# A fused retention and two-layer MLP kernel on one core: another order of its opening, another rate of weight conversion for layer 2, and a whole last output block

## The chip, the cores and the metric

The kernel runs on one core of a Trainium2 chip. The metric is device time in microseconds (us) from launch to end, as a median of several runs; the profile gives the span from the first to the last instruction of one execution, which is a little shorter. PE is TensorE (matmuls), DVE is VectorE, ACT is ScalarE, POOL is GpSimd, SP is SyncE, which here only issues DMAs.

## The reference

Retention over 2 sequences with 8 heads, 768 positions and head width 64, then two feed-forward layers over the 1536 resulting rows of width 512. Both hidden widths are 2048.

```python
gamma = 1.0 - 2.0 ** (-5.0 - np.arange(H))
for t in range(S):
    state = gamma * state + outer(k[:, :, t], v[:, :, t])
    y[:, :, t] = (1 / sqrt(D)) * einsum('bhd,bhde->bhe', q[:, :, t], state)
x = y.transpose(0, 2, 1, 3).reshape(B * S, H * D)
h = x @ moe_w_in;   x = elu(h) @ moe_w_out
h = x @ moe2_w_in;  out = softplus(h) @ moe2_w_out
```

q, k and v are float32, the four weight matrices are float64 in memory, the output is float32.

## The kernel before

**Retention by tiles.** The 1536 positions are 12 tiles of 128, six to a sequence; four tiles make a block of 512 rows. A tile j goes through these helpers. `load_tile` (L68) issues three DMAs of 256 KB on SP's queue, q, k and v. `ret_prep` (L197) scales v by a decay, on DVE for the first four tiles and on POOL for the rest. `ret_transpose` (L201) transposes q and k on PE, four 128x128 pieces each; DVE then copies q out of PSUM while it multiplies by the query decay `gq` (L216), and ACT copies k out (L214). `ret_scores` (L243) forms the 128x128 score blocks of the eight heads in 16 matmuls, and DVE multiplies them by the causal mask into the tile A (L252), of which there is one buffer. `ret_state` (L225) forms k'v in 16 matmuls, and DVE folds it into the running state `st` (L237 to L240). `ret_wide` (L219) has POOL copy that state into a block-diagonal tile `wide`. `ret_out` (L256) is eight matmuls of `wide` (not for the first tile of a sequence) and 16 of A with v into one bank; ACT writes the rounded high half xh (L276) and DVE the rest xl (L277).

**Matrix products by units.** 96 units follow: 2 layers, 3 blocks of 512 rows, 16 slices of 128 hidden columns. Every operand is split into a high part, rounded by ACT, and a low part, subtracted by DVE (`split_w`, L158 to L167, for weights; `act_split`, L325, for activations), and each product is three passes. `hidden(u)` (L293) is 12 matmuls of 512 columns: w_hi x_hi, w_hi x_lo, w_lo x_hi. `act(u)` (L303) is ELU in layer 1 (two ACT and one DVE instruction) and softplus in layer 2 (three ACT and four DVE). `project(u)` (L333) is another 12 matmuls into four accumulators. In the loop over u at L452, `hidden` and `act` run two units ahead of `project`. In layer 1 one retention job of a tile 4 to 11 (transposes, scores, or output with state) is put in each unit from u = 1 on.

**Weights.** `load_w` (L128) brings a 128x512 float64 slice (512 KB) into one of five `raw` buffers; `conv_w` (L139) turns it into float32 with two ACT instructions (L150, L151) and two DVE instructions (L152, L153). `wq` (L379) is the order of the slices, and `next_conv` (L393) converts the next slice if its place is free and then issues the load of one more. A layer-2 slice becomes free when the last block of layer 1 has split the layer-1 slice in that place, from u = 29 on. In a unit the first `next_conv(1)` stands behind `hidden`, and a second call stands at the unit's end (L467): always for layer-1 weights, and for layer-2 weights only if u is even.

**Order of the work.** Nothing is scheduled by a planner: each engine runs its instructions in the order in which the program lists them, and DMAs of one queue are issued in program order. The opening is the code from L399 to L439. SP issues tiles 0 and 1 (L85, L86), then a weight slice, tile 2, a slice, tile 3, three slices, tiles 4 and 5. In the opening the masks (L252) of tile s-1 are multiplied between the two transposes of tile s, and `ret_out(s - 1)` comes in the same step:

```python
    for s in range(TPB):
        ret_transpose(s, (0,))
        ...
        if s:
            ret_scores(s - 1)
        ret_transpose(s, (1,))
        ret_wide(s)
        ret_state(s)
        ...
        if s:
            ret_out(s - 1)
```

`gq` is made on the chip: ACT's queue loads 2x512 decays and a 2x128 selector, one matmul (L115) spreads them over 128 partitions, DVE copies the result. `keep_clock` (L106) issues matmuls on a zeroed tile, 8 at the start and 4 in the first step of the opening. At the end `finish` (L353) copies the four output blocks of 128 rows out of PSUM, ACT for even and DVE for odd ones, the very last one in two halves, one by each engine, and SP's queue writes them out.

Of the kernel before, what the change touches and what calls it, by code (L numbers as in the profile page):

```python
# [19 lines left out]
P = 128  # L20
# [3 lines left out]
def tile_retention_elu_softplus(  # L24
# [43 lines left out]
    def load_tile(j):  # L68
        b, c = divmod(j, CPB)
        r = []  # L70
        for n, (src, nm) in enumerate(((q, "q"), (k, "k"), (v, "v"))):
            t = early[n][:, j] if j < TPB else rp.tile([P, H, D], F32, tag=nm, name=nm)
            nc.sync.dma_start(out=t, in_=src[b, :, c * P:(c + 1) * P, :].rearrange("h s d -> s h d"))
            r.append(t)
        qkv[j] = r
# [3 lines left out]
    decq = gp.tile([2, HP * P], F32, tag="gh", name="decq")  # L79
    sel = gp.tile([2, P], F32, tag="gl", name="sel")  # L80
    dec = const.tile([P, H + HP], F32, name="dec")
    nc.scalar.dma_start(out=decq, in_=decay_q[:, 0:HP * P])
    nc.scalar.dma_start(out=sel, in_=decay_q[:, HP * P:])
    nc.scalar.dma_start(out=dec, in_=decay)
    load_tile(0)  # L85
    load_tile(1)  # L86
# [23 lines left out]
    keep_clock(8)  # L110


    gq = const.tile([P, HP * P], F32, name="gq")
    gb = ps.tile([P, 512], F32, tag="r1", name="gb")
    nc.tensor.matmul(gb, sel, decq, start=True, stop=True)  # L115
    nc.vector.tensor_copy(gq, gb)
# [80 lines left out]
    def ret_prep(j):  # L197
        vt = qkv[j][2]
        (nc.vector if j < TPB else nc.gpsimd).tensor_tensor(out=vt, in0=vt, in1=gv, op=ALU.mult)
# [43 lines left out]
    def ret_scores(j):  # L243
# [6 lines left out]
        a = ap.tile([P, 2, HP, P], F32, tag="A", name="A")  # L250
        for i in range(2):
            nc.vector.tensor_tensor(out=a[:, i], in0=bs[i].rearrange("p (h t) -> p h t", h=HP),  # L252
                                    in1=mask.unsqueeze(1).to_broadcast([P, HP, P]), op=ALU.mult)
        scores[j] = a

    def ret_out(j):  # L256
# [11 lines left out]
        for pr in range(HP):  # L268
            for i in range(2):
                o = i * D  # L270
                nc.tensor.matmul(b[o:o + D, pr * P:(pr + 1) * P], vt[:, 2 * pr + i, :], a[:, i, pr, :],  # L271
# [21 lines left out]
    def hidden(u):  # L293
# [4 lines left out]
        seq = [(ah, xh, kk) for kk in range(KK)] + [(ah, xl, kk) for kk in range(KK)] + [(al, xh, kk) for kk in range(KK)]  # L298
# [53 lines left out]
    def finish(u):  # L352
# [3 lines left out]
        for i in range(4):  # L356
# [4 lines left out]
            else:  # L361
                o = rp.tile([P, DM], F32, tag="qk"[i // 2], name="o")
                r = blk * TB + i * P
                if u == NU - 1 and i == 3:
                    nc.scalar.activation(out=o[:, :DM // 2], in_=acc[i][:, :DM // 2], func=AF.Copy)
                    nc.vector.tensor_copy(o[:, DM // 2:], acc[i][:, DM // 2:])
                elif i % 2:
# [3 lines left out]
                nc.sync.dma_start(out=out[r:r + P, :], in_=o)  # L371
# [26 lines left out]

    next_load(1)  # L399
    load_tile(2)  # L400
    next_load(1)
    load_tile(3)
    next_load(3)
    load_tile(4)
    load_tile(5)
    cv = list(wq)

    for s in range(TPB):
        ret_transpose(s, (0,))
        if s == 0:  # L410
            ret_prep(0)
        if s:
            ret_scores(s - 1)
        ret_transpose(s, (1,))
        ret_wide(s)
        ret_state(s)
        if s == 0:
            keep_clock(4)
        ret_prep(s + 1)
        if s:  # L420
            next_conv(1)
        if s > 1:
            split_w(s - 2, 0)
        if s:
            ret_out(s - 1)
    ret_scores(TPB - 1)
    ret_wide(TPB)
    ret_out(TPB - 1)
    rot["banks"] = ["r0", "r1"]
# [9 lines left out]
    next_conv(1)  # L439
# [12 lines left out]
    for u in range(NU):  # L452
# [14 lines left out]
        if not cv or cv[0][0] == 0 or u % 2 == 0:  # L467
# [3 lines left out]
def _decay(H, D):  # L471
    gamma = [1.0 - 2.0 ** (-5.0 - h) for h in range(H)]
    HP = H // 2
    d = np.zeros((P, H + HP), dtype=np.float32)
    dq = np.zeros((2, HP * P + P), dtype=np.float32)
    for h, g in enumerate(gamma):
        d[D * (h % 2):D * (h % 2 + 1), H + h // 2] = g ** P
        dq[h % 2, HP * P + D * (h % 2):HP * P + D * (h % 2 + 1)] = 1.0
        for t in range(P):
            d[t, h] = g ** -(t + 1)  # L480
            dq[h % 2, P * (h // 2) + t] = g ** (t + 1) / float(D) ** 0.5
    return d, dq
# [28 lines left out]
```

## Time and profile before

| what | value |
|---|---|
| time, median of 3 runs | 604.85 us (603.58 to 986.68) |
| the profiled execution's own time | 605.01 us |
| its span | 602.5 us |
| busy in the span: PE, DVE, ACT, POOL | 591.9, 466.5, 415.5, 22.4 us |
| mean granted TensorE clock | 0.995 |

The profile is of one execution. Its own time is 2.5 us longer than its span (start and end outside the instructions), and 0.16 us above the median. Busy time of an engine is the time in which at least one of its instructions ran; matmuls overlap, so a busy PE need not be PE at its full rate.

### The profile page before, as it was taken

The page shows a single profiled execution, that of the slowest core. Times are in us where ns is not written, and L with a number is a line of the kernel's source. Part 1 is how long each engine was busy: PE and PEld are TensorE (multiplying, and loading weights), DVE is VectorE, ACT ScalarE, POOL GpSimd, SP SyncE. Part 2 cuts the span into 40 slices and gives each one's busy share as a digit, 9 for nine tenths or more (in the row PEclk, how much of TensorE's full clock was granted, in tenths as well). Part 3 has the DMA queues.
Part 4 walks back from the last instruction along what each step waited for, and adds up shares of the span by engine and source line. Part 5 has one row for each costly group of instructions (what it writes and reads, how often), then busy time and mean ns, then how long its engine had stood idle before and what let it go on. Part 6 is the DMA issues. An engine that isn't in the chain of part 4 may idle for free.

```text
span 602.5 us, 8184 instructions
## 1 busy us (share of the span) xinstructions
PE 591.9 (98%) x3038; PEld 484.1 (80%) x3038; DVE 466.5 (77%) x746; ACT 415.5 (69%) x700; POOL 22.4 (4%) x38
## 2 busy tenths in 40 slices
PE   8999999999999999999999999999999999999997
PEld 4777888888888888888888877888888888888885
DVE  3969999865655545888888999978877887878774
ACT  1569888844644456898888977766776667766763
POOL 1200100110111000000000000000000000000000
PEclk9989999999999999999999999999999999999999
DMA  9966768750110000344454200000100000100001
GB/s 208 265 193 204 179 209 234 206 136 18 41 36 1 1 0 2 105 140 144 136 158 157 105 1 1 1 0 1 70 2 1 0 1 0 71 0 2 0 1 70
DMA packets 60863, 46.67 MB, mean 77 GB/s; under 512 B 38804, under 2 KB 55190, under 8 KB 60824
## 3 DMA queue, kind: packets, MB, share of 16 engines
q1 hardware_dynamic: 60672, 46.14, 26.9%
q8 instruction: 24, 0.39, 0.3%
q14 instruction: 15, 0.12, 0.1%
q10 hardware_dynamic: 152, 0.01, 0.0%
HBM read 43.00 MB, written 3.15 MB: 77 GB/s over the span
## 4 chain that ended last, share of the span: by engine, by line
PE 87%; DVE 6%; ACT 5%; issue 1%; DVEq 0%; ACTq 0%
PE h L300 39%; PE a L350 34%; PE r L350 6%; PE r L248 1%; PE r L271 1%; DVE cl L152 1%; PE r L265 1%; PE r L207 1%; PE wb L108 1%; ACT cl L151 1%; ACT wh L164 1%; ACT cm L150 1%; DVE A L252 1%; DVE wl L165 1%; DVE wo L153 1%
## 5 line engine op out<-in xcount | busy, mean ns | idle before, releaser
L300 PE MATMUL h<-xh,wh 128*128 128x512 f32 x384 | 103.6, 392 | 1.7 <-ACT xh L276 0.7
L300 PE MATMUL h<-xh,wl 128*128 128x512 f32 x384 | 103.2, 390 | 0.5 <-DVE wl L165 0.5
L300 PE MATMUL h<-xl,wh 128*128 128x512 f32 x384 | 103.5, 392 | 0.0
L300 PEld LDWEIGHTS h<-xh,wh 128*128 128x128 f32 x384 | 72.1, 188 | 17.6 <-ACT wh L164 0.9
L164 ACT ACTIVATE wh<-wo 128x512 fp32r<-128x512 f32 x96 | 60.4, 629 | 37.1 <-PE a L350 33.5
L300 PEld LDWEIGHTS h<-xh,wl 128*128 128x128 f32 x384 | 72.2, 188 | 16.4 <-DVE wl L165 1.4
L300 PEld LDWEIGHTS h<-xl,wh 128*128 128x128 f32 x384 | 72.7, 189 | 15.2
L165 DVE TENSOR_TENSOR wl<-wo,wh 128x512 fp32r<-128x512 f32 x96 | 67.3, 701 | 17.1 <-ACT wh L164 17.0
L165 DVE TENSOR_TENSOR wl<-wi,wh 128x512 fp32r<-128x512 f32 x96 | 66.6, 693 | 0.0
L164 ACT ACTIVATE wh<-wi 128x512 fp32r<-128x512 f32 x96 | 59.4, 619 | 0.0
L350 PE MATMUL a<-gh,wh 128*128 128x512 f32 x192 | 57.0, 404 | 0.0
L350 PE MATMUL a<-gh,wl 128*128 128x512 f32 x192 | 54.4, 390 | 0.0
L350 PE MATMUL a<-gl,wh 128*128 128x512 f32 x192 | 54.3, 389 | 0.0
L329 ACT ACTIVATE gh<-w 128x512 fp32r<-128x512 f32 x48 | 30.4, 632 | 34.1 <-DVE w L321 33.9
L152 DVE SCALAR_TENSOR_TENSOR cl<-cm,cl 128x512 int32<-128x512 int32 x64 | 45.0, 702 | 10.9 <-ACT cl L151 10.8
L315 ACT ACTIVATE e<-h 128x512 f32<-128x512 f32 x48 | 28.6, 595 | 30.3 <-PE h L300 30.3
L151 ACT ACTIVATE cl<-raw,half 128x512 int32<-128x512 uint32 x64 | 48.0, 750 | 0.1
L318 DVE TENSOR_SCALAR w<-e 128x512 f32<-128x512 f32 x48 | 20.4, 426 | 34.7 <-ACT e L316 34.6
L310 DVE SCALAR_TENSOR_TENSOR e<-e,h 128x512 f32<-128x512 f32 x48 | 32.8, 683 | 18.8 <-ACT e L309 18.6
L150 ACT ACTIVATE cm<-raw 128x512 f32<-128x512 f32 x64 | 42.3, 660 | 0.3 <-DVE cl L152 0.3
L350 PEld LDWEIGHTS a<-gh,wl 128*128 128x128 f32 x192 | 36.1, 188 | 7.8
L350 PEld LDWEIGHTS a<-gl,wh 128*128 128x128 f32 x192 | 36.0, 188 | 7.6
(121 smaller groups left out, 912.4 us busy)
## 6 DMA issues: line engine op xcount, KB each, us to landing
raw<-moe_w_in SPq DMA_DIRECT2D x32, 512.0 KB, 3.8
raw<-moe_w_out SPq DMA_DIRECT2D x32, 512.0 KB, 3.3
out_dram<-o SPq DMA_DIRECT2D x12, 256.0 KB, 2.0
q<-q SPq DMA_DIRECT2D x8, 256.0 KB, 5.2
k<-k SPq DMA_DIRECT2D x8, 256.0 KB, 4.5
v<-v SPq DMA_DIRECT2D x8, 256.0 KB, 6.4
xl<-q SPq DMA_DIRECT2D x4, 256.0 KB, 5.1
xh<-k SPq DMA_DIRECT2D x4, 256.0 KB, 5.1
```

The costliest lines, as they stand in the source:

```text
L108: nc.tensor.matmul(wb, warm[:, 0:P], warm, start=True, stop=True)
L150: nc.scalar.activation(out=m, in_=hi.bitcast(F32), func=AF.Copy, scale=2.0 ** -112)
L151: nc.scalar.activation(out=l, in_=lo.bitcast(U32), func=AF.Relu, scale=2.0 ** -29, bias=half)
L152: nc.vector.scalar_tensor_tensor(out=l, in0=m.bitcast(I32), scalar=3, in1=l, op0=ALU.logical_shift_left, op1=ALU.bitwise_or)
L164: nc.scalar.activation(out=h, in_=a, func=AF.Copy)
L165: nc.vector.tensor_tensor(out=l, in0=a, in1=h.bitcast(F32), op=ALU.subtract)
L300: nc.tensor.matmul(b, w[:, kk, :], x[:, kk, :], start=(n == 0), stop=(n == len(seq) - 1))
L310: nc.vector.scalar_tensor_tensor(out=e, in0=e, scalar=-1.0, in1=h, op0=ALU.add, op1=ALU.max)
L315: nc.scalar.activation(out=e, in_=h, func=AF.Abs)
L318: nc.vector.tensor_scalar(out=w, in0=e, scalar1=1.0, scalar2=-1.0, op0=ALU.add, op1=ALU.add)
L329: nc.scalar.activation(out=gh, in_=g, func=AF.Copy)
L350: nc.tensor.matmul(acc[i], st[:, i * P:(i + 1) * P], mv, start=(f == 0 and p == 0), stop=(f == NF - 1 and p == 2))
```

## The change

Eight edits. (1) The query decay is a full 128x512 array in memory and comes by one DMA on SP's queue, between k and v of tile 0; its two small DMAs, matmul and copy go, and with them one dummy matmul of eight. (2) All of tiles 0 to 3 is loaded first, then five weight slices, then tile 4; tile 5 is issued at the opening's end. (3) The opening's loop issues both transposes of a tile, then scores of tile s, output of tile s-1, transposes of tile s+1, state, wide, prep; the four dummy matmuls inside go. (4) `ret_prep` is on POOL for every tile. (5) A is two tiles, which for tiles 0 to 3 lie in the triple-buffered `gh` and `gl`. (6) Two conversions instead of three precede `hidden(0)`; `hidden(0)` runs the pass with x_lo last. (7) Layer-2 slices get a second conversion in three of four units. (8) The last output block is copied whole by ACT, which also issues its DMA.

```diff
--- before.py
+++ after.py
@@ -69,6 +69,8 @@
         b, c = divmod(j, CPB)
         r = []
         for n, (src, nm) in enumerate(((q, "q"), (k, "k"), (v, "v"))):
+            if j == 0 and n == 2:
+                nc.sync.dma_start(out=gq, in_=decay_q)
             t = early[n][:, j] if j < TPB else rp.tile([P, H, D], F32, tag=nm, name=nm)
             nc.sync.dma_start(out=t, in_=src[b, :, c * P:(c + 1) * P, :].rearrange("h s d -> s h d"))
             r.append(t)
@@ -76,14 +78,11 @@
 
     early = [xpool.tile([P, TPB, H, D], F32, tag=t, name=t) for t in ("xl2", "xh2", "xl1")]
     early_t = xpool.tile([P, 4, HP, P], F32, tag="xh1", name="xh1")
-    decq = gp.tile([2, HP * P], F32, tag="gh", name="decq")
-    sel = gp.tile([2, P], F32, tag="gl", name="sel")
     dec = const.tile([P, H + HP], F32, name="dec")
-    nc.scalar.dma_start(out=decq, in_=decay_q[:, 0:HP * P])
-    nc.scalar.dma_start(out=sel, in_=decay_q[:, HP * P:])
+    gq = const.tile([P, HP * P], F32, name="gq")
     nc.scalar.dma_start(out=dec, in_=decay)
-    load_tile(0)
-    load_tile(1)
+    for j in range(TPB):
+        load_tile(j)
     gv = dec[:, 0:H].unsqueeze(2).to_broadcast([P, H, D])
     gs = dec[:, H:H + HP].unsqueeze(2).to_broadcast([P, HP, D])
 
@@ -107,13 +106,7 @@
         for _ in range(n):
             nc.tensor.matmul(wb, warm[:, 0:P], warm, start=True, stop=True)
 
-    keep_clock(8)
-
-
-    gq = const.tile([P, HP * P], F32, name="gq")
-    gb = ps.tile([P, 512], F32, tag="r1", name="gb")
-    nc.tensor.matmul(gb, sel, decq, start=True, stop=True)
-    nc.vector.tensor_copy(gq, gb)
+    keep_clock(7)
 
 
     wf = [(wres.tile([P, KK, P], F32, name=f"wi{f}"), wres.tile([P, DM], F32, name=f"wo{f}")) for f in range(NF)]
@@ -196,7 +189,7 @@
 
     def ret_prep(j):
         vt = qkv[j][2]
-        (nc.vector if j < TPB else nc.gpsimd).tensor_tensor(out=vt, in0=vt, in1=gv, op=ALU.mult)
+        nc.gpsimd.tensor_tensor(out=vt, in0=vt, in1=gv, op=ALU.mult)
 
     def ret_transpose(j, parts=(0, 1)):
         for n in parts:
@@ -247,9 +240,12 @@
             for i in range(2):
                 nc.tensor.matmul(bs[i][:, pr * P:(pr + 1) * P], kT[i * D:(i + 1) * D, pr, :], qT[i * D:(i + 1) * D, pr, :],
                                  start=(pr == 0), stop=(pr == HP - 1), skip_group_check=True)
-        a = ap.tile([P, 2, HP, P], F32, tag="A", name="A")
+        if j < TPB:
+            a = [gp.tile([P, HP, P], F32, tag=t, name="A") for t in ("gh", "gl")]
+        else:
+            a = [ap.tile([P, HP, P], F32, tag=t, name="A") for t in ("A0", "A1")]
         for i in range(2):
-            nc.vector.tensor_tensor(out=a[:, i], in0=bs[i].rearrange("p (h t) -> p h t", h=HP),
+            nc.vector.tensor_tensor(out=a[i], in0=bs[i].rearrange("p (h t) -> p h t", h=HP),
                                     in1=mask.unsqueeze(1).to_broadcast([P, HP, P]), op=ALU.mult)
         scores[j] = a
 
@@ -268,7 +264,7 @@
         for pr in range(HP):
             for i in range(2):
                 o = i * D
-                nc.tensor.matmul(b[o:o + D, pr * P:(pr + 1) * P], vt[:, 2 * pr + i, :], a[:, i, pr, :],
+                nc.tensor.matmul(b[o:o + D, pr * P:(pr + 1) * P], vt[:, 2 * pr + i, :], a[i][:, pr, :],
                                  start=(first and pr == 0), stop=(pr == HP - 1), skip_group_check=True)
         xh, xl = slot(j // TPB)
         c = slice((j % TPB) * P, (j % TPB + 1) * P)
@@ -295,7 +291,8 @@
         xh, xl = slot(blk)
         ah, al = ws.pop((u, 0))
         b = psum(f"h{u % 2}")
-        seq = [(ah, xh, kk) for kk in range(KK)] + [(ah, xl, kk) for kk in range(KK)] + [(al, xh, kk) for kk in range(KK)]
+        passes = [(ah, xh), (ah, xl), (al, xh)] if u else [(ah, xh), (al, xh), (ah, xl)]
+        seq = [(w, x, kk) for w, x in passes for kk in range(KK)]
         for n, (w, x, kk) in enumerate(seq):
             nc.tensor.matmul(b, w[:, kk, :], x[:, kk, :], start=(n == 0), stop=(n == len(seq) - 1))
         hb[u] = b
@@ -361,14 +358,11 @@
             else:
                 o = rp.tile([P, DM], F32, tag="qk"[i // 2], name="o")
                 r = blk * TB + i * P
-                if u == NU - 1 and i == 3:
-                    nc.scalar.activation(out=o[:, :DM // 2], in_=acc[i][:, :DM // 2], func=AF.Copy)
-                    nc.vector.tensor_copy(o[:, DM // 2:], acc[i][:, DM // 2:])
-                elif i % 2:
+                if i % 2 == (u < NU - 1):
                     nc.vector.tensor_copy(o, acc[i])
                 else:
                     nc.scalar.activation(out=o, in_=acc[i], func=AF.Copy)
-                nc.sync.dma_start(out=out[r:r + P, :], in_=o)
+                (nc.scalar if u == NU - 1 and i == 3 else nc.sync).dma_start(out=out[r:r + P, :], in_=o)
 
 
     LOOK = 2
@@ -396,36 +390,28 @@
                 conv_w(*cv.pop(0))
                 next_load(1)
 
-    next_load(1)
-    load_tile(2)
-    next_load(1)
-    load_tile(3)
-    next_load(3)
+    next_load(5)
     load_tile(4)
-    load_tile(5)
     cv = list(wq)
 
+    ret_transpose(0)
+    ret_prep(0)
     for s in range(TPB):
-        ret_transpose(s, (0,))
-        if s == 0:
-            ret_prep(0)
-        if s:
-            ret_scores(s - 1)
-        ret_transpose(s, (1,))
-        ret_wide(s)
-        ret_state(s)
-        if s == 0:
-            keep_clock(4)
-        ret_prep(s + 1)
-        if s:
+        ret_scores(s)
+        if s == TPB - 1:
             next_conv(1)
-        if s > 1:
-            split_w(s - 2, 0)
         if s:
             ret_out(s - 1)
-    ret_scores(TPB - 1)
-    ret_wide(TPB)
+        if s + 1 < TPB:
+            ret_transpose(s + 1)
+        ret_state(s)
+        ret_wide(s + 1)
+        ret_prep(s + 1)
+    split_w(0, 0)
+    next_conv(1)
     ret_out(TPB - 1)
+    split_w(1, 0)
+    load_tile(5)
     rot["banks"] = ["r0", "r1"]
     rot["i"] = 0
     hidden(0)
@@ -436,7 +422,7 @@
     split_w(0, 1)
     act_split(0)
     act(1)
-    next_conv(1)
+    next_conv(2)
     loaded = TPB + 2
 
     def job():
@@ -464,22 +450,21 @@
         if u + LOOK < NU:
             act(u + LOOK)
         finish(u)
-        if not cv or cv[0][0] == 0 or u % 2 == 0:
+        if not cv or cv[0][0] == 0 or u % 4 < 3:
             next_conv(2 if u in (0, 5) else 1)
 
 
 def _decay(H, D):
     gamma = [1.0 - 2.0 ** (-5.0 - h) for h in range(H)]
-    HP = H // 2
-    d = np.zeros((P, H + HP), dtype=np.float32)
-    dq = np.zeros((2, HP * P + P), dtype=np.float32)
+    d = np.zeros((P, H + H // 2), dtype=np.float32)
+    dq = np.zeros((P, H // 2, P), dtype=np.float32)
     for h, g in enumerate(gamma):
-        d[D * (h % 2):D * (h % 2 + 1), H + h // 2] = g ** P
-        dq[h % 2, HP * P + D * (h % 2):HP * P + D * (h % 2 + 1)] = 1.0
+        r = slice(D * (h % 2), D * (h % 2 + 1))
+        d[r, H + h // 2] = g ** P
         for t in range(P):
             d[t, h] = g ** -(t + 1)
-            dq[h % 2, P * (h // 2) + t] = g ** (t + 1) / float(D) ** 0.5
-    return d, dq
+            dq[r, h // 2, t] = g ** (t + 1) / float(D) ** 0.5
+    return d, dq.reshape(P, -1)
 
 
 def kernel(q, k, v, moe_w_in, moe_w_out, moe2_w_in, moe2_w_out):
```

## Rows read from the trace of the kernel before

**Rows 1.** The page's chain that ended last, shares of the span by engine.
```profile
PE 87%; DVE 6%; ACT 5%; issue 1%; DVEq 0%; ACTq 0%
```
**Rows 2.** Timeline: first matmuls of hidden(0), and scores of tile 4, with idle before.
```profile
33.37 1.81 PE L300 MATMUL h<-xh,wh 128*128 128x512 f32 x4 [0.69 <-ACT xh L276]
...
56.10 1.16 PE L248 MATMUL r<-qT,kT 64*128 64x128 f32 x16 [0.91 <-DVE qT L216]
```
**Rows 3.** Windows: length, busy PE, PEld, DVE, ACT, POOL, then PEclk, DMA share, GB/s.
```profile
4.00:9.00 5.00, 4.75 (x12) 2.07 (x10) 1.76 (x3) 0.21 (x1) 0.00 (x0) 1.00 1.32 219
...
30.00:33.40 3.40, 1.90 (x21) 1.23 (x19) 1.59 (x4) 0.68 (x2) 1.38 (x3) 1.00 0.99 258
33.40:37.80 4.40, 4.40 (x12) 3.46 (x13) 3.32 (x5) 2.35 (x4) 0.00 (x0) 0.61 0.73 241
```
**Rows 4.** Timeline of PE in the first 12 us: start, length, instructions.
```profile
1.25 3.60 PE L108 MATMUL wb<-warm 128*128 128x512 bf16 x8 [1.25 <-DVE warm L103]
...
7.69 1.06 PE L207 MATMUL h<-ident,xh 128*128 128x128 f32 x4
...
9.28 1.12 PE L232 MATMUL a<-xl,xh 128*64 128x64 f32 x16 [0.53 <-DVE xl L199]
...
10.33 1.89 PE L108 MATMUL wb<-warm 128*128 128x512 bf16 x4
```
**Rows 5.** Timeline of SP, and the DMA view's time to landing: k of tile 0.
```profile
1.30 0.57 SPq L73 DMA_DIRECT2D xh<-k  x1
...
xh<-k SPq DMA_DIRECT2D x1, 256.0 KB, 4.2
```
**Rows 6.** Timeline of the opening from 17 to 33 us: one instruction group of each kind.
```profile
17.30 1.16 PE L248 MATMUL a<-qT,kT 64*128 64x128 f32 x16
...
19.60 1.16 PE L265 MATMUL h<-qT,wide 128*128 128x128 f32 x8
...
24.56 0.68 DVE L277 TENSOR_TENSOR xl<-h,xh 128x512 fp32r<-128x512 f32 x1
...
25.16 0.67 DVE L216 TENSOR_TENSOR xh<-h,gq 128x512 f32<-128x512 f32 x1
...
31.60 1.09 PE L271 MATMUL a<-A,xl 128*64 128x128 f32 x14 [0.16 <-DVE A L252]
...
32.72 0.60 ACT L276 ACTIVATE xh<-a 128x512 fp32r<-128x512 f32 x1 [3.92 <-PE a L271]
```
**Rows 7.** Timeline of POOL; then line 199 on DVE: ns min, median, max.
```profile
21.98 1.51 POOL L223 COPY wide<-st 64x256 f32<-64x256 f32 x2 [3.88 <-DVE st L240]
...
29.38 1.27 POOL L199 TENSOR_TENSOR v<-v,dec 128x512 f32<-128x512 f32 x1 [5.89 <-DMA v<-v]
...
L199 DVE TENSOR_TENSOR xl<-xl,dec x4: 680/682/685, 8.5 to 21.7; 128x512 f32<-128x512 f32 x4
```
**Rows 8.** The page's groups of the conversion: busy us, mean ns, idle before.
```profile
L152 DVE SCALAR_TENSOR_TENSOR cl<-cm,cl 128x512 int32<-128x512 int32 x64 | 45.0, 702 | 10.9 <-ACT cl L151 10.8
...
L151 ACT ACTIVATE cl<-raw,half 128x512 int32<-128x512 uint32 x64 | 48.0, 750 | 0.1
...
L150 ACT ACTIVATE cm<-raw 128x512 f32<-128x512 f32 x64 | 42.3, 660 | 0.3 <-DVE cl L152 0.3
```
**Rows 9.** Windows: ten units of block 3 in layer 1, five units of layer 2.
```profile
267.00:321.40 54.40, 54.40 (x241) 45.06 (x240) 45.26 (x71) 46.63 (x81) 0.00 (x0) 1.00 0.45 145
...
372.00:399.20 27.20, 27.20 (x122) 22.53 (x121) 24.41 (x40) 19.73 (x33) 0.00 (x0) 1.00 0.00 1
```
**Rows 10.** Timeline of PE: first pass of hidden(52), and of hidden(55), in layer 2.
```profile
350.43 1.07 PE L300 MATMUL h<-xh,wh 128*128 128x512 f32 x4
...
369.47 1.07 PE L300 MATMUL h<-xh,wh 128*128 128x512 f32 x4
```
**Rows 11.** Timeline of the end: the last output block's two half copies.
```profile
598.15 0.38 ACT L365 ACTIVATE o<-a 128x256 f32<-128x256 f32 x1
598.57 0.42 DVE L366 COPY o<-a 128x256 f32<-128x256 f32 x1 [1.08 <-ACT o L365]
```

## Prediction

> **What bounds the kernel now.** I read the page's chain first: 87% of the span is PE's own work, 6% DVE, 5% ACT [rows 1]. So only stretches in which PE waits, or runs slowly, can give anything. In steady state ten units take 54.4 us with PE never idle [rows 9], 5.44 us a unit, and 96 units of this are 522 us; retention jobs and the opening make most of the rest. The timeline of PE and the windows show four places outside that rate. First, `hidden(0)` begins only at 33.37 us [rows 2]. Second, PE was busy for just 1.90 of the 3.4 us ahead of it, and then its clock fell: granted 0.61 in the mean of 33.4 to 37.8 us, where the 12 matmuls of `hidden(0)` took 4.4 us [rows 3] in place of a half unit's 2.72, so 1.7 us were lost. Third, the scores of tile 4 waited 0.91 us for qT [rows 2], with ACT and DVE behind. Fourth, `hidden(52)` to `hidden(55)` took 369.47 - 350.43 = 19.04 us [rows 10] for three units, which at 5.44 take 16.32: 2.7 us lost. The end has one row of note: two half copies one after the other [rows 11].
>
> **The opening (edits 1 to 6).** PE runs at 1.2 GHz at first: eight dummies of 512 columns take 3.60 us [rows 4], 0.45 each. The granted-clock column reads 1.00 there [rows 3], so the durations must be trusted. It is still so in the second dummy burst at 10.33 us, four in 1.89 us [rows 4].
>
> What goes: the decay's matmul and copy, which stood between the first dummies and the transposes, and four dummies, 1.89 us [rows 4]. What comes: one 256 KB DMA for `gq` ahead of v of tile 0 and ahead of all later tiles. At 219 GB/s [rows 3] a 256 KB load takes 1.2 us; this is the upper bound for `gq`, and half of it the lower, since its rows are longer than q's. The weights, before in between, now come behind tile 3. k of tile 0 lands at 1.30 + 4.2 = 5.5 us [rows 5], `gq` by 6.7, v by 7.9, then nine loads of 1.2: tile 3 is complete at about 18.7, the first weight near 20.5. Each is ahead of its use below, so the loads are hidden; the margin for k of tile 3 (17.5, transposed at about 19) is only 1.5 us.
>
> Now the chain in the new order, with durations by kind. k of tile 0 at 5.5, transposes at 1.2 GHz 1.06 [rows 4], copy by ACT 0.60 [rows 6]: scores(0) at 7.2. Its length at 1.2 GHz no row shows; the bounds are 1.16 [rows 6] and twice that, and I take 2.0, near the upper, as the neighbours run at that clock. Transposes of tile 1, nearly twice 1.06, then state(0) 1.12 [rows 4]: scores(1) at 12.2. From there each step is a loop through three engines: scores 1.16, outputs of the tile before 1.1, xh 0.60, xl 0.68, and qT of the next tile behind that xl on DVE, 0.67 [rows 6]: 4.2 us, so scores(2) at 16.4. From the second on the wide matmuls add 1.16 [rows 6]: 5.4, scores(3) at 21.8. The last step runs over POOL, where `ret_prep` now stands behind `ret_wide`: state on DVE about 0.9 (an estimate: two instructions of half a tile), wide 1.51, prep 1.27 [rows 7], state(3) 0.7 (an estimate, from 1.12 at the lower clock [rows 4]), wide and output matmuls 2.26, xh 0.60 [rows 6]: 7.2 us, and `hidden(0)` begins at 29.0 if PE is at full clock from 12 us on. If it rises one step later, scores(1) and out(0) cost twice their 2.26, and it begins at 31.2. I take 29.8, nearer the first, because the dense burst from 7 to 12 is like the stretch after which the clock rose before. That is 3.6 us earlier than 33.4.
>
> Moving prep to POOL costs 1.27 in place of 0.68 [rows 7], but takes 0.68 off DVE for each tile; it is on the path in the last step alone. GPSIMD Engine Reference of the Trainium skill, section Engine selection, speaks against this move: a two-input product belongs on VectorE and takes about twice as long on GpSimd. By it prep is 1.36 and `hidden(0)` 0.1 us later; by the row, 1.27, the ratio is 1.9.
>
> Next, PE has no idle stretch like that of rows 3 ahead of `hidden(0)`: between scores(3) and it PE has some 5.5 us of work in 7.2. I expect no fall of the clock, so `hidden(0)` takes 2.72: 1.7 us more. The pass order of `hidden(0)` puts x_lo last, so xl of tile 3, behind a conversion on DVE, is covered by two passes, two thirds of 2.72; without this cover it would cost up to 0.7.
>
> What is late next is ACT and DVE. One conversion (ACT 0.66 + 0.75, DVE twice 0.70 [rows 8]) is moved from ahead of `hidden(0)` to behind it, while PE passes that stretch 1.7 us quicker. They already hold PE for 0.91 us at the scores of tile 4 [rows 2]. If they had slack for both, nothing is paid; if for neither, 1.4 + 1.7 = 3.1 us. Between these I take 1.1, since ACT and DVE had idle time in 33.4 to 37.8 (2.35 and 3.32 busy of 4.4 [rows 3]) that can be used. Sum of the opening: 3.6 + 1.7 - 1.1 = 4.2 us gained. Bounds: 0.8 lost for a flat PE as below, 6.8 gained with an early clock.
>
> The two-tile A removes a wait only where the next scores come before the old output; for tiles 4 to 11 the outputs come a unit earlier, so nothing.
>
> **Layer-2 conversion (edit 7).** By the code the 32 conversions start at u = 29. Before, 24 are done after unit 45, and eight fall in units 46 to 50; after, 28 are done by then, and four remain (46 to 48). A layer-2 unit without them has DVE busy for 24.41 / 5 = 4.88 us [rows 9]; a conversion adds 1.40 [rows 8]. Five units with eight: 24.4 + 11.2 = 35.6 against 27.2 of PE, 8.4 too much, of which 2.7 were lost [rows 10]: the work ahead covers 5.7. With four: 30.0, 2.8 too much, which is covered. So all of the 2.7 comes back. The price lies earlier: ten units of layer 1 with 15 conversions have ACT 46.63 and DVE 45.26 of 54.4 busy [rows 9]; 2.5 more add 3.5 each: 50.2 and 48.8 still fit, so nothing is paid there. Bounds: 0 and 2.7 gained.
>
> **The end (edit 8).** 598.15 to 598.99 for two halves [rows 11] becomes one copy of 0.60 [rows 6]: 0.2 us. The DMA's issue moves from SP to ACT; nothing is queued behind it. Bounds 0 and 0.5.
>
> **Sum.** 605.0 (the execution's own time; the median is 604.85, so the two need no correction) - 4.2 - 2.7 - 0.2 = 597.9 us.
>
> **Rivals.**
> 1. *PE stays at half clock up to `hidden(0)`.* The four dummies that went are those after which it rose. For it: 3.60 us of dummies and a stretch of 4.75 busy of 5 did not raise it [rows 3, 4]. Against it: slow matmuls fill their own gaps. PE's share of the chain from scores(1), 2.3 + 3.4 + 6.4 = 12 us, would nearly double; less the waits that it fills, `hidden(0)` starts near 38.5, 5.1 later than before; ACT and DVE then hold nothing up (0.9 back): 4.2 lost, 605.0 + 4.2 - 2.7 - 0.2 = 606.3, slower than before. It decides for slower once `hidden(0)` starts after about 37 us. TensorE: Matmul & The Clock Gate of the Trainium skill, Part 1, says that an idle engine runs at half its rate and reaches the full one only after it was kept busy for a while; by it, gaps in the new opening lead to this rival's 606.3. The trace of before agrees as to the fall after 30 us, less so at the start.
> 2. *The clock rises late, or falls again.* `hidden(0)` near 32 and slow as before: 1.4 gained, 600.7.
> 3. *ACT and DVE take the gain.* The whole 4.5 (3.1 and a longer queue of 1.4) is waited for in the first units: 0.8 gained, 601.3. For it: the 0.91 of rows 2. Against it: their idle time in rows 3.
> 4. *Layer 2 keeps its loss*, if not the number of conversions but softplus alone holds PE there: 605.0 - 4.2 - 0.2 = 600.6. Against it: five later units run at 5.44 [rows 9].
>
> **Chances.** Forecast 0.50; rivals 0.08, 0.20, 0.12, 0.10. The range reaches down to an early clock, `hidden(0)` at 27.3, 2.5 more: 595.4, and up past rivals 2 to 4 to 602.0, leaving rival 1 out. A measurement of this kernel tells about 2% (12 us) from no change; no case reaches it: faster 0.03, same 0.95, slower 0.02.
>
> **What would show it.** Right: `hidden(0)` at 29 to 31 us with a granted clock near 1; matmuls at full rate from 12 to 16 us; a wait of PE of 1 to 3 us before the scores of tile 4; 5.44 a unit through `hidden(52)` to `hidden(55)`; the last conversion in unit 48. Wrong: transposes of 1.06 us beyond 20 us, `hidden(0)` after 33, or waits of PE on ACT in 267 to 321 us.

## The result, and the profile after

The changed kernel takes 597.09 us as a median of four runs (596.85 to 598.43), against 604.22 for the kernel before beside it, a median that counts one slow execution of 986.68 us; without it the ratio is 0.9891, 95% interval 0.9866 to 0.9915. The forecast was 597.9, the range 595.4 to 602.0. The profiled execution took 598.43 us, its span is 596.7. So 6.6 us went between the two profiled executions: 5.8 in the span, 0.8 outside it (605.01 - 602.5 = 2.5 before, 1.7 after).

The times of one kernel fall into two groups some 1.5 us apart, and experiment 11 comes to their cause. The kernel before mostly takes 602.9 to 603.7 (603.15 in what follows) and now and then 604.8 to 605.0; the changed kernel takes 596.9 (once 597.3) or 598.4. Both profiled executions are of the upper group. Differences below are taken between like groups where that matters.

The page's chain that ended last, of the changed kernel, by engine:

```profile
PE 95%; DVE 2%; ACT 1%; DMA 1%; issue 1%; SPq 0%; DVEq 0%; ACTq 0%
```

PE's share is 95%, where it was 87 [rows 1]. The timeline of the changed kernel (start, length, instructions, idle time before and its releaser) at the places that the prediction spoke of:

```profile
4.14 0.63 PE L200 MATMUL h<-ident,xl 128*128 128x128 f32 x4
...
6.97 1.75 PE L241 MATMUL a<-qT,kT 64*128 64x128 f32 x16 [1.06 <-DVE qT L209]
...
10.74 0.69 PE L225 MATMUL r<-xl,xh 128*64 128x64 f32 x16
11.50 1.16 PE L241 MATMUL h<-qT,kT 64*128 64x128 f32 x16
...
21.19 1.16 PE L241 MATMUL r<-xh 64*128 64x128 f32 x16 [0.47 <-DVE xh L209]
...
27.73 1.20 PE L297 MATMUL h<-xh,wh 128*128 128x512 f32 x4 [0.70 <-ACT xh L272]
...
34.48 1.17 PE L297 MATMUL h<-xh,wh 128*128 128x512 f32 x4 [0.99 <-ACT wh L157]
...
51.57 1.96 PE L241 MATMUL r<-qT,kT 64*128 64x128 f32 x16 [1.87 <-DVE qT L209]
...
57.07 1.07 PE L297 MATMUL h<-xh,wh 128*128 128x512 f32 x4
...
347.45 1.09 PE L297 MATMUL h<-xh,wh 128*128 128x512 f32 x4
...
363.81 1.07 PE L297 MATMUL h<-xh,wh 128*128 128x512 f32 x4
...
592.49 0.60 ACT L364 ACTIVATE o<-a 128x512 f32<-128x512 f32 x1 [0.76 <-PE a L347]
```

The windows of the changed kernel: length, busy time (instructions) of PE, PEld, DVE, ACT and POOL, then granted clock, DMA share, GB/s:

```profile
45.00:60.00 15.00, 12.99 (x61) 10.24 (x60) 14.79 (x24) 14.55 (x26) 0.00 (x0) 0.89 0.69 211
51.50:53.50 2.00, 1.93 (x17) 1.74 (x17) 1.97 (x4) 2.00 (x5) 0.00 (x0) 0.56 0.67 197
262.00:316.00 54.00, 54.00 (x240) 44.72 (x239) 48.21 (x77) 48.88 (x85) 0.00 (x0) 1.00 0.56 176
340.00:366.00 26.00, 26.00 (x116) 21.41 (x115) 24.93 (x42) 18.68 (x32) 0.00 (x0) 1.00 0.00 1
```

And two lines of the kernel before: `hidden(5)` in PE's timeline, and the window 50 to 55 us.

```profile
60.08 1.07 PE L300 MATMUL h<-xh,wh 128*128 128x512 f32 x4
...
50.00:55.00 5.00, 5.00 (x23) 3.95 (x22) 4.90 (x9) 4.97 (x10) 0.00 (x0) 1.00 0.76 244
```

Read them in order of time. `hidden(0)` begins at 27.73, where it was 33.37 [rows 2]: 5.6 us earlier. Two waits of PE follow, 0.99 before `hidden(2)` and 1.87 at the scores of tile 4 (0.91 before [rows 2]), and behind the second the clock falls: granted 0.56 in the window from 51.5 us, the scores take 1.96 in place of 1.16. By `hidden(5)` only 3.0 of the 5.6 us are left (it begins at 57.07, before at 60.08). Nothing more changes until layer 2. There `hidden(52)` to `hidden(55)` take 363.81 - 347.45 = 16.36, where they took 19.04 [rows 10]: 2.7 more. The end gives 0.15, what is left of the 5.8: one copy of 0.60 in place of two halves [rows 11].

The windows say why. In 45 to 60 us DVE is busy for 14.79 and ACT for 14.55 of 15 us, PE for 12.99: here PE waits and the other two have almost no idle time. In 262 to 316 us, with more conversions than before, ACT has 48.88 and DVE 48.21 of 54, and PE has no gap.

So the theory to test: layer 2 gives 2.65 by the rate alone; the new order of the opening gives 5.6 us at `hidden(0)`, and ACT and DVE take some 3 of it back; the rest of the edits are worth nothing. Open: what the 0.8 us outside the span are, and what part each opening edit has.

### The profile page after: what moved, and what is told of

It is laid out like the page before. It is cut to its first block, busy times and chain, and to the rows that moved or that the text cites. A ratio compares the mean times of both kernels' runs of the same rounds, so it can differ in the third digit from the quotient of the medians.

```text
span 596.7 us, 8178 instructions
## 1 busy us (share of the span) xinstructions
PE 584.9 (98%) x3031; PEld 482.0 (81%) x3031; DVE 463.9 (78%) x741; ACT 415.3 (70%) x699; POOL 24.9 (4%) x42
## 3 DMA queue, kind: packets, MB, share of 16 engines
HBM read 43.26 MB, written 3.15 MB: 78 GB/s over the span
## 4 chain that ended last, share of the span: by engine, by line
PE 95%; DVE 2%; ACT 1%; DMA 1%; issue 1%; SPq 0%; DVEq 0%; ACTq 0%
PE h L297 42%; PE a L347 37%; PE r L347 7%; PE r L241 2%; PE r L267 1%; PE r L200 1%; PE r L261 1%; DMA gq<-decay_q 1%; DVE cl L145 1%; PE r L225 0%; PE a L200 0%; PE a L241 0%; DVE wi L146 0%; PE h L241 0%; DVE wo L146 0%
```

## Experiments

Diffs are against the changed kernel if nothing else is said.

**1. Layer 2's rate undone.**

```diff
-        if not cv or cv[0][0] == 0 or u % 4 < 3:
+        if not cv or cv[0][0] == 0 or u % 2 == 0:
```

> The changed kernel with the second layer-2 conversion again only in even units. Theory (two separate gains, opening and layer 2): the 2.7 us lost over hidden(52) to hidden(55) come back, the last conversion is in unit 50, and the time is 2.7 us above the changed kernel, near 599.8. Rival (the opening's shift, not the rate, removed the loss, because everything reaches layer 2 in another phase): those units stay at 5.44 us each and the time stays near 597.

Measured: 600.96 us, ratio 0.9954 [0.9942, 0.9966]; the groups are 599.6 and 601.0, so 2.6 to 2.7 above those of the changed kernel; the profiled execution is of the lower group. The timeline of PE in this run, of the opening (for experiment 2) and of that stretch, and its window:

```profile
27.38 1.21 PE L297 MATMUL h<-xh,wh 128*128 128x512 f32 x4 [0.70 <-ACT xh L272]
...
34.60 1.16 PE L297 MATMUL h<-xh,wh 128*128 128x512 f32 x4 [1.44 <-ACT wh L157]
...
51.67 1.16 PE L241 MATMUL r<-qT,kT 64*128 64x128 f32 x16 [1.85 <-DVE qT L209]
...
55.63 1.07 PE L297 MATMUL h<-xh,wh 128*128 128x512 f32 x4
...
345.98 1.07 PE L297 MATMUL h<-xh,wh 128*128 128x512 f32 x4
352.67 1.17 PE L297 MATMUL h<-xh,wh 128*128 128x512 f32 x4 [0.49 <-DVE w L317]
358.90 1.20 PE L297 MATMUL h<-xh,wh 128*128 128x512 f32 x4 [0.51 <-ACT wh L157]
364.99 1.07 PE L297 MATMUL h<-xh,wh 128*128 128x512 f32 x4
```
```profile
340.00:366.00 26.00, 24.47 (x105) 18.99 (x104) 25.03 (x41) 19.27 (x34) 0.00 (x0) 1.00 0.00 1
```

The three units, 345.98 to 364.99, take 19.01 again, with two named waits. DVE is as busy as with the new rate (25.03 and 24.93 of 26 us), but now PE has gaps: 24.47 in place of 26.00. The edit's value depends on nothing in the opening.

**2. The rate alone, on the kernel before.**

```diff
-        if not cv or cv[0][0] == 0 or u % 2 == 0:
+        if not cv or cv[0][0] == 0 or u % 4 < 3:
```

> The kernel before with only the layer-2 rate changed. Theory: 2.7 us less than before, near 601.5, with nothing lost in units 29 to 45. Rival (ACT or DVE is overfull at 1.75 conversions a unit and gives part of it back earlier): over 602.5, with PE waiting between 230 and 325 us.

Measured: 600.5 us against 603.15, ratio 0.9953 [0.9941, 0.9964]: 2.65 us, the same from the other side. This run and the last also show the opening by itself: one has the old opening, the other the new one, and neither lost its clock after `hidden(0)`. PE's timeline of this run:

```profile
33.53 1.19 PE L300 MATMUL h<-xh,wh 128*128 128x512 f32 x4 [0.69 <-ACT xh L276]
...
54.66 1.16 PE L248 MATMUL r<-qT,kT 64*128 64x128 f32 x16 [0.90 <-DVE qT L216]
...
58.63 1.07 PE L300 MATMUL h<-xh,wh 128*128 128x512 f32 x4
```

Beside it stand the first four lines of experiment 1. There `hidden(0)` is 6.15 us earlier (33.53 - 27.38) and `hidden(5)` 3.00 (58.63 - 55.63): the new opening is worth 3.0 us, and 3.15 are paid back on the way, 1.44 and 1.85 - 0.90 of it in two named waits, the rest in smaller gaps. By the times it is somewhat less: 603.15 - 599.6 and 600.5 - 596.9 are 3.6 us, which less 0.75 outside the span and 0.15 at the end leaves 2.7; this profiled execution, 600.88, is the slowest of its five.

**3. The end undone:** the last block in two halves again, its DMA on SP.

```diff
-                if i % 2 == (u < NU - 1):
+                if u == NU - 1 and i == 3:
+                    nc.scalar.activation(out=o[:, :DM // 2], in_=acc[i][:, :DM // 2], func=AF.Copy)
+                    nc.vector.tensor_copy(o[:, DM // 2:], acc[i][:, DM // 2:])
+                elif i % 2:
...
-                (nc.scalar if u == NU - 1 and i == 3 else nc.sync).dma_start(out=out[r:r + P, :], in_=o)
+                nc.sync.dma_start(out=out[r:r + P, :], in_=o)
```

> The changed kernel with the last output block in two halves again and its DMA on SP. The profiled execution of before lies 2.5 us above its span, that of the changed kernel 1.7. Theory: the end is worth the 0.2 us of the copy alone, time near 597.3, and the time outside the span stays near 1.7. Rival: the last DMA's queue sets how late the program counts as ended, so the time outside the span goes back to 2.5 and the time is 1.0 above the changed kernel, near 598.1.

Measured: 598.42 us, ratio 0.9906 [0.9892, 0.992], in groups of 596.9 to 597.0 and 598.4 to 598.6: 0 to 0.2 us above the changed kernel's. Its profiled execution has 598.62 - 596.9 = 1.7 us outside the span, like the changed kernel's. So the last DMA's queue isn't what the 0.8 us came from.

**4. `ret_prep` of the first four tiles back on DVE.**

```diff
-        nc.gpsimd.tensor_tensor(out=vt, in0=vt, in1=gv, op=ALU.mult)
+        (nc.vector if j < TPB else nc.gpsimd).tensor_tensor(out=vt, in0=vt, in1=gv, op=ALU.mult)
```

> The changed kernel with the v products of tiles 0 to 3 on DVE again. Theory (after the opening ACT and DVE hold PE, so a start of hidden(0) that is a little earlier or later is made up in the waits before hidden(2) and the scores of tile 4): hidden(0) moves by up to 0.5 us, the time by less than 0.3. Rival (POOL's product and wide copy set the opening): the time falls by 0.5 us or more.

Measured: 599.25 us, ratio 0.9934 [0.9923, 0.9946], 2.2 above the changed kernel's median. PE's timeline:

```profile
8.01 1.25 PE L241 MATMUL a<-qT,kT 64*128 64x128 f32 x16 [1.97 <-DVE qT L209]
...
22.15 1.16 PE L241 MATMUL r<-xh 64*128 64x128 f32 x16 [0.47 <-DVE xh L209]
...
28.69 1.20 PE L297 MATMUL h<-xh,wh 128*128 128x512 f32 x4 [0.70 <-ACT xh L272]
...
53.80 2.07 PE L347 MATMUL a<-gh,wh 128*128 128x512 f32 x4
```

From scores(3) to `hidden(0)` it is 6.54 us, exactly as with POOL (27.73 - 21.19): the product isn't on the path in that step on either engine. The whole opening is shifted by the 1.0 us by which the first scores are late, and here the decay array landed later (5.2 us after issue, 4.1 in the changed kernel). It isn't made up in the waits that follow, as the theory had it: the scores of tile 4 begin at 52.50, 0.93 later than in the changed kernel. This execution, too, lost its clock behind that wait (2.07 for the first matmuls of `project(2)`), so it compares with the profiled one of the changed kernel: 600.09 - 598.43 = 1.7 us, 1.0 of it in the span (597.7 and 596.7), which is the shift, and 0.7 outside it (2.4 and 1.7). The 2.4 outside the span stands in all five executions (2.39 to 2.45), as in the kernel before, so the 0.7 comes back with the product on DVE. What made the array late here stays open, and so does whether the other four executions had the shift, the lost clock or both.

**5. The decay array first on ACT's queue.**

```diff
-            if j == 0 and n == 2:
-                nc.sync.dma_start(out=gq, in_=decay_q)
...
+    nc.scalar.dma_start(out=gq, in_=decay_q)
     nc.scalar.dma_start(out=dec, in_=decay)
```

> The changed kernel with the query decay's 256 KB issued first on ACT's queue instead of third on SP's. In the changed kernel qT of tile 0 waits for it until 6.1 us, and one run had it as late as 7.1. Theory (the decay's landing starts the chain that ends in hidden(0), and a shift passes on whole): it lands earlier, scores(0) begins at 6.5 or before, hidden(0) and the time fall by 0.3 to 1.0 us. Rival (transposes and copy of k are as late, 7.2 in the run without a wait for the decay): within 0.3 us.

Measured: 599.93 us, ratio 0.9934 [0.9921, 0.9947], 2.8 above the changed kernel's median. The profiled executions of both lost their clock behind the scores of tile 4, and between these it is 1.5 (599.93 and 598.43). PE's timeline:

```profile
5.33 1.09 PE L199 MATMUL h<-ident,xl 128*128 128x128 f32 x4 [0.91 <-DMA xl<-q]
...
8.32 2.08 PE L240 MATMUL a<-qT,kT 64*128 64x128 f32 x16 [0.69 <-ACT kT L206]
```

The decay array was early, but now q of tile 0 was late (4.4 us after issue in place of 3.2): the first transposes wait for its DMA, and the first scores come at 8.32 in place of 6.97. They take 2.08 in place of 1.75, and `hidden(0)` begins at 29.51, 1.8 later. The theory fell. Two queues gave the loads no second path. The Trainium skill, Trainium Kernel Development and Optimization, section Key Constraints, says just that: DMAs issued from SP, ACT and POOL all run on the same engines, and more issuing engines save only the time to issue. The trace agrees, with q's 1.2 us.

**6. Three more dummy matmuls behind the first transposes.**

```diff
     ret_transpose(0)
+    keep_clock(3)
     ret_prep(0)
```

> The changed kernel with three dummy matmuls between the transposes of tile 0 and scores(0), where PE waits 1.1 us. Theory (the clock fell at about 7 us because of that wait, so scores(0) and two transposes ran at half rate, 0.6 and 0.9 us late): full rate from the dummies on, hidden(0) 0.5 to 1.3 us earlier, time lower by as much. Rival (the level in the first 10 us is set by when the rise comes in a run, not by these gaps): no difference beyond the spread of the runs, 596.9 to 598.4.

Measured: 597.04 us, ratio 0.9896 [0.9881, 0.991]: nothing, as the rival said. `hidden(0)` began at 27.63, yet the scores of tile 4 at 51.92, later than in the changed kernel. The timeline of DVE and POOL in this run shows a likely reason:

```profile
30.62 0.69 DVE L145 SCALAR_TENSOR_TENSOR cl<-cm,cl 128x512 int32<-128x512 int32 x1 [0.51 <-ACT cl L144]
30.73 1.50 POOL L192 TENSOR_TENSOR v<-v,dec 128x512 f32<-128x512 f32 x1 [2.54 <-DMA v<-v]
31.35 1.42 DVE L146 SCALAR_TENSOR_TENSOR wi<-raw,cl 128x512 int32<-128x512 int32 x1
```

Beside POOL's product of tile 4 DVE's conversion takes 1.42 us in place of 0.69, on the chain that PE then waits for (1.47 before `hidden(2)`). The profiled executions of experiments 1 and 9 have the same: the conversion beside the product takes 1.42 and 1.51, and the wait is 1.44 and 1.54; in the changed kernel's it takes 0.94, and the wait is 0.99. No experiment took this product away, so its share is argued, not shown.

**7. Dummy matmuls in the wait before the scores of tile 4,** into the first of the two banks.

```diff
         bs = [rbank(), rbank()]
+        if j == TPB:
+            z = ident.bitcast(BF16)
+            for _ in range(12):
+                nc.tensor.matmul(bs[0][:, 0:2 * P], z[:, 0:P], z, start=True, stop=True)
```

> The changed kernel with twelve short dummy matmuls in the wait of PE before the scores of tile 4. Its runs fall into two groups, 596.9 and 598.4. Theory (in the second group the clock falls in that wait, and scores and project(2) take 1.5 us longer): with the dummies all runs are in the first group, near 596.9, and the scores take 1.16 us. Rival (the groups come from the first 10 us): both groups are still there.

Measured: 598.19 us, ratio 0.991 [0.9896, 0.9923]. PE's timeline:

```profile
51.60 1.47 PE L242 MATMUL r<-ident 128*128 128x256 bf16 x12 [1.76 <-DVE qT L209]
53.00 1.16 PE L245 MATMUL r<-qT,kT 64*128 64x128 f32 x16
```

They came behind the wait, not into it: that bank is free only once DVE has copied q out of it. So the run tells one thing alone: 1.4 us of work put on PE's path there made the kernel 1.3 us slower than the changed kernel's lower group. PE is the bound from that place on. None of its four executions (598.14 to 598.29) is 1.5 us above the others.

**8. The first conversion a step earlier.**

```diff
-        if s == TPB - 1:
+        if s >= TPB - 2:
             next_conv(1)
...
-    next_conv(2)
+    next_conv(1)
```

> The changed kernel with a conversion also in the third step of the opening, as before three ahead of hidden(0), one fewer behind hidden(1). Theory (ACT and DVE set the time from 25 to 52 us, the order of their work matters little, its amount is the same): hidden(0) 1 to 3.5 us later, the waits before hidden(2) and the scores of tile 4 shorter by nearly as much, the time within 1 us of the changed kernel. Rival (an early hidden(0) is a gain of its own): the time is higher by what hidden(0) is later, over 1.5 us.

Measured: 600.37 us, ratio 0.9946 [0.9934, 0.9959], 3.5 above the changed kernel's lower group. The timeline of ACT and PE:

```profile
20.74 0.66 ACT L143 ACTIVATE cm<-raw 128x512 f32<-128x512 f32 x1 [5.75 <-DMA raw<-moe_w_in]
...
24.83 2.08 PE L241 MATMUL r<-xh 64*128 64x128 f32 x16 [4.47 <-DVE xh L209]
...
34.06 1.20 PE L297 MATMUL h<-xh,wh 128*128 128x512 f32 x4 [0.70 <-ACT xh L272]
```

The first weight lands only at 20.7 us, behind all of tiles 0 to 3. ACT, with the conversion next in its queue, stood still for 5.75 us, DVE's part of the conversion stood before the copy of q, which began at 24.00, and PE waited 4.47, after which the clock was low. `hidden(0)` came 6.3 us later than in the changed kernel. Of this 3.5 us reached the end by the medians; in the profiled execution, 601.12, it is 4.2. So between a third and a half of a shift of `hidden(0)` is made up behind it, in experiments 1 and 2 half.

**9 and 10. The retention job ahead of the conversion in each unit; in 10 also no second conversion in unit 0.**

```diff
-        next_conv(1)
         job()
+        next_conv(1)
         project(u)
```
```diff
-            next_conv(2 if u in (0, 5) else 1)
+            next_conv(2 if u == 5 else 1)
```

> The changed kernel with a unit's retention job listed ahead of its first conversion, so that qT and the masks of tile 4 and later stand before that conversion on DVE. PE's order is the same. Theory (DVE is full from 25 to 57 us, and PE's 1.9 us wait at the scores of tile 4 is the place of qT in DVE's queue): the wait falls to about 0.8 us, the time by 1.0 to 1.4 against runs of the first group (596.9), and no run of the second group (598.4) is left. Rival (ACT or the weight loads hold the chain, so the wait only moves to the next hidden): less than 0.5 us.

> As the run before, and the extra conversion at the end of unit 0 is left out, so that the conversions run just ahead of need. Theory: DVE has 1.3 us less to do before the scores of tile 4, the wait falls to some 0.3 us, the time is 2.0 to 2.6 us under the changed kernel's first group, near 594.6. Rival (too little is converted ahead, PE waits for a weight in units 1 to 6): no lower than the run before.

Measured: 595.83 us, ratio 0.9879 [0.9866, 0.9893], and 594.76 us, ratio 0.9859 [0.9844, 0.9874]. PE's timelines at the scores of tile 4 and `hidden(5)`, of 9 and of 10:

```profile
50.30 1.16 PE L241 MATMUL r<-qT,kT 64*128 64x128 f32 x16 [0.54 <-DVE qT L209]
...
54.26 1.07 PE L297 MATMUL h<-xh,wh 128*128 128x512 f32 x4
```
```profile
27.92 1.20 PE L297 MATMUL h<-xh,wh 128*128 128x512 f32 x4 [0.70 <-ACT xh L272]
...
35.26 1.17 PE L297 MATMUL h<-xh,wh 128*128 128x512 f32 x4 [1.54 <-ACT wh L157]
...
49.96 1.16 PE L241 MATMUL r<-qT,kT 64*128 64x128 f32 x16
...
53.91 1.07 PE L297 MATMUL h<-xh,wh 128*128 128x512 f32 x4
```

The wait of 1.87 us becomes 0.54 and then almost nothing, though not one instruction less is done: qT stood behind a conversion that PE needed only later. From `hidden(0)` to `hidden(5)` it is 28.25 us in experiment 1 and 25.10 with the old opening of experiment 2; here it is 27.00 (54.26 - 27.26) and 25.99 (53.91 - 27.92). So of the 3.15 paid back in experiment 1, 2.3 came from the order and the timing of the feeders' work, not from its amount. Experiment 10 is the fastest kernel of all, 2.3 us under the changed kernel by medians. Its remaining wait, 1.54 before `hidden(2)`, is for a weight that isn't yet converted; its profiled execution, at 595.71, is the slowest of its four.

**11. The dummies of 7 into the other bank,** which ACT's copy of k frees.

```diff
+                nc.tensor.matmul(bs[1][:, 0:2 * P], z[:, 0:P], z, start=True, stop=True)
```

> The changed kernel with the twelve dummy matmuls written to the other bank of the tile-4 scores, the one that ACT's copy of k frees at 49.4 us, so that they run inside PE's wait. Theory (the second group of runs, 1.5 us higher, is the clock falling in that wait): all runs near 596.9. Rival (the second group has another cause): both groups are still there, near 596.9 and 598.4.

Measured: 596.84 us (596.59 to 596.98), ratio 0.9894 [0.9881, 0.9908]. PE's timeline:

```profile
49.71 1.49 PE L242 MATMUL r<-ident 128*128 128x256 bf16 x12
51.62 1.16 PE L245 MATMUL r<-qT,kT 64*128 64x128 f32 x16 [0.43 <-DVE qT L209]
```

Now the dummies lie inside the wait. The scores begin when they did, but at full rate, and none of four executions is in the 598.4 group. The cause of the groups is seen in profiled executions of either kind, here of experiment 3 (598.62, upper group) and of experiment 6 (597.21, lower):

```profile
51.82 1.91 PE L241 MATMUL r<-qT,kT 64*128 64x128 f32 x16 [1.83 <-DVE qT L209]
```
```profile
51.92 1.16 PE L241 MATMUL r<-qT,kT 64*128 64x128 f32 x16 [1.88 <-DVE qT L209]
```

The wait is nearly the same, but only in the upper group do the scores behind it run slowly; so it is in the changed kernel (1.96) against experiment 1 (1.16, lower group). The sizes agree: from the scores of tile 4 to `hidden(5)` it is 57.07 - 51.57 = 5.50 us in the changed kernel's profile and 55.63 - 51.67 = 3.96 in experiment 1's, a difference of 1.54, that of the groups. The other executions fit: in the 20 of the changed kernel and experiments 1, 3 and 6, the mean granted clock is 0.997 or less in each of the nine of an upper group, and 0.998 or more in each of the eleven of a lower one. The second group is the clock falling behind that wait, in some executions and not in others. That the dummies prevent the fall is likely but not shown: four executions are few where 11 of 20 escape anyway, and experiment 7, whose wait is as long as before, has none of four either. Experiments 9 and 10, whose wait is 0.54 us or less, have none of eight, which speaks for the wait as what brings the fall about.

**12. The decay by DMA alone, on the kernel before** (edit 1 with its one dummy less; its short form):

```diff
+            if j == 0 and n == 2:
+                nc.sync.dma_start(out=gq, in_=decay_q)
...
-    keep_clock(8)
-    gb = ps.tile([P, 512], F32, tag="r1", name="gb")
-    nc.tensor.matmul(gb, sel, decq, start=True, stop=True)
-    nc.vector.tensor_copy(gq, gb)
+    keep_clock(7)
```

> The kernel before with the first edit alone: the query decay by one 256 KB DMA between k and v of tile 0, no matmul, copy or small DMAs for it, seven dummies at the start. Theory (the start of the chain is one part of the opening's gain, the new order of loads and loop another): hidden(0) 0.5 to 2 us before 33.4, its clock still falling, the time 0.5 to 2 us lower. Rival (the whole gain of the opening is this edit): hidden(0) below 30 us and the time 3 us lower. Also: time outside the span 2.5 as before, or 1.7 if the small DMAs make that difference.

Measured: 603.39 us in 11 runs, ratio 1.0004 [0.9995, 1.0013]. PE's timeline:

```profile
8.04 0.69 PE L225 MATMUL a<-xl,xh 128*64 128x64 f32 x16 [1.84 <-DVE xl L192]
...
15.88 1.16 PE L241 MATMUL a<-qT,kT 64*128 64x128 f32 x16
...
33.45 1.20 PE L293 MATMUL h<-xh,wh 128*128 128x512 f32 x4 [0.69 <-ACT xh L269]
```

And DVE's longest wait between 8 and 34 us (in total, times, longest), which the kernel before does not have:

```profile
DVE xl L192 <- DMA xl<-v: 3.5, 3, 1.6
```

In the end nothing is gained, though the chain starts earlier: state(0) begins at 8.04 (before 9.28 [rows 4]), in spite of its wait for the product of v, and the scores of tile 1 at 15.88 (before 17.30 [rows 6]). But with 256 KB more ahead of them, v of tiles 1 to 3 come late for DVE, which waits 3.5 us for them, and `hidden(0)` is where it was. So edit 1 alone, with the old order of loads, is worth nothing. The opening's 3 us come from its other edits, or from edit 1 together with them; the order of loads, the loop and the product on POOL, which takes the wait for v off DVE, weren't separated further. Outside the span this run has 603.19 - 600.8 = 2.4 us, like the kernel before.

## Why the prediction was right

**Layer 2 (predicted 2.7).** Measured 2.65 from both sides (experiments 1 and 2). The reasoning by budgets held too: the last conversion falls in unit 48, and the stretch that bears the additional conversions has no gap of PE.

**The end (predicted 0.2).** 0.15 in the trace; experiment 3 can't tell it from nothing.

**The opening (predicted 4.2).** The net is 2.7 to 3.0, by experiments 1 and 2 and by the two profiles. Two terms were off, on opposite sides:
- *The start.* "I take 29.8" for `hidden(0)`; it was 27.73, outside the 29 to 31 named as a sign. The loop's steps were right: 4.30 from scores(1) at 11.50 to scores(2) at 15.80 (4.2 predicted), and 5.39 from there to scores(3) (5.4). Of the 2.1 us, 0.8 was the allowance for a late clock, not needed, since full rate held from 10.74 us to `hidden(0)` and beyond; 0.6 was there at scores(3) already; and 0.7 was the last step, 6.54 in place of 7.2, whose way over POOL isn't on the path (experiment 4). One wait was not counted: in this execution qT of tile 0 is held by the decay array, which landed at 6.0 us, not by k's copy; the prediction's own 6.7 for the array, with 0.67 for qT, would have put scores(0) at 7.4 and not 7.2.
- *The payment.* "Between these I take 1.1" for ACT and DVE; they took 3.15 in experiment 1, the prediction's own price for no slack at all (3.1), and in the profiled execution 1.5 more through the clock. This is the step that failed. The idle time of ACT and DVE in 33.4 to 37.8 us [rows 3] was taken as room for the moved work; but 15 us later, where the stage is tightest, they had none: already in the kernel before DVE was busy for 4.90 and ACT for 4.97 of the 5 us from 50 on. The window that decides is that of the tightest stretch, not of the place where the work is put. Nor was the order in their queues looked at, on which 2.3 of the 3.15 hung (experiments 9 and 10). Rival 3 (all 4.5 us taken) was nearer in kind than the forecast allowed, though too big.
- *The clock.* The 1.7 us that `hidden(0)` lost at half clock are gone, but they were a trait of the profiled execution: the old opening in experiment 2 doesn't lose them. In their place the changed kernel loses its clock in some executions behind the wait for the scores of tile 4.

**Outside the span (nothing predicted).** 0.7 to 0.8 us less. It goes with edit 4: 1.7 to 1.8 in every execution of every kernel that has the v products of tiles 0 to 3 on POOL, and 2.4 to 2.6 in every execution of those that have them on DVE, the kernel before, experiments 2 and 12, and experiment 4, which has the new opening with this one edit undone. Experiment 3 excludes the last DMA's queue, experiment 12 the decay's DMA. By what way the place of the product acts there is open.

For the usual groups it adds up, to the few tenths by which such sums differ: 3.0 (opening) + 2.65 (layer 2) + 0.15 (end) + 0.75 (outside) = 6.55, and 603.15 - 596.9 = 6.25. So the layer-2 part was right for its reasons, but the sum came out right in part by luck: a start that was 2 us too cautious, and 0.75 us nobody had seen, offset a backlog that was 2 us too cheap. Rival 1 (half clock up to `hidden(0)`) fell: with four dummies less the first transposes already ran at full rate (0.63 at 4.14 us), the clock was low again at scores(0) (1.75; granted 0.50 from 8 to 10 us), and from 10.74 us on full rate held up to `hidden(0)`. Rival 2 (slow clock in `hidden(0)`) fell with the 1.20 at 27.73. Rival 4 fell with experiment 2.

## What to carry to other kernels

Starting the bounding engine earlier is worth only what its feeders can follow: here half of it came back as waits, and the window of the tightest stage ahead, 50 to 55 us of the kernel before, could have shown that beforehand. Then look at the order in the feeders' queues: putting what the bounding engine waits for ahead of work that is needed later gave 1.1 us for no work at all, and one conversion less in the tight unit 0 another 1.1. Last, look at single executions: here a wait of 1.9 us cost 3.4 where the clock fell behind it, and that one wait made the changed kernel's two groups of times.

## What the hardware showed that was not expected

- DVE's two-input conversion took 1.42 us in place of 0.69 beside POOL's product of v (experiment 6), where the product took 1.50 in place of 1.05, and 0.94 in the changed kernel, where the two overlapped by 0.4 us only. GPSIMD Engine Reference of the Trainium skill, section Specifications, says that GpSimd shares its interfaces to SBUF with VectorE and contends with DVE instructions that have two inputs there; the trace agrees.
- The granted-clock record reads 1.00 while the first dummy matmuls run at 0.45 us per 512 columns [rows 3, 4], half the rate of later ones: the 12 matmuls of 512 columns of `hidden(5)` take 2.72, 0.23 each. The time at which full rate was first seen differed between nearly equal kernels: 4.1 us in the changed kernel, where it was lost again at 7 and came back at 10.7, 7.4 in experiment 6, about 13.3 in experiment 5.
